# Attention, expert layer and feed-forward on one core: softmax sums and one-hot rank masks moved from VectorE to GpSimd

## The chip, the cores and the metric

The kernel runs on 1 core of a Trainium2 chip. The metric is the time of one execution on the device, in microseconds; the time before is the median of 3 runs. PE is TensorE, DVE is VectorE, ACT is ScalarE, POOL is GpSimd; SP only issues DMAs here.

## The reference

Three stages follow each other. The change touches the first, causal attention with a learned decay, and its end, where the tokens get their experts.

```python
B, H, S, D = 4, 8, 576, 64
bias = -(cum[:, :, :, None] - cum[:, :, None, :])          # cum: running sum of max(s, 0)
scores = np.where(causal, -1e9, scores + np.minimum(bias, 0.0))
attn = np.exp(scores - scores.max(-1, keepdims=True))
attn = attn / (attn.sum(-1, keepdims=True) + 1e-9)
x = attn @ v                                               # 2304 tokens x 512
...
e_idx = np.argmax(x @ w_gate, axis=1)                      # one of 8 experts per token
h = np.maximum(x[mask] @ w1[e], 0.0); ye = h @ w2[e]       # per expert, times gate weights
...
r = np.maximum(x @ w_in, 0.0); out = (r * r) @ w_out       # 512 -> 2048 -> 512
```

## The kernel before

Attention goes over 16 pairs of heads (4 batches of 4 pairs; `pp` is the pair). A pair is cut into 7 units (blocks of 128 query rows, with the last 64 rows of both heads in one unit). For each unit PE makes scores (L636), DVE adds the mask, negates and finds the row extreme (L663), ACT exponentiates and sums the rows into one column of `rs` (L680), PE transposes the weights (L696), ACT or DVE copies them out of PSUM (L715, L717). PE then multiplies with `v` (L733), in two halves of a pair: half 0 is row blocks 0 and 1, half 1 the rest. The sums of a pair lie in `rs_t[pp % 2]`, so a pair after next overwrites them.

`emit_rc` turns the sums of one half into factors: for half 1 it first moves the sums of the tail rows of the second head from partitions 64 to 127 down to 0 to 63 (L759), then adds 1e-9 (L760) and takes the reciprocal in place (L762). `emit_xe` (L806) multiplies the transposed output of the half with them, and after every fourth pair L858 uses them for the gate logits. All five are on DVE.

After each batch `emit_gate` finds each token's expert and its rank among that expert's tokens. `s_rk` (L940) gives the ranks, `s_r1` (L945) makes for each of 5 row blocks a one-hot mask of 128x384: `iota_r` (fp16) compared with the rank, written as bf16. `s_tb` (L955) multiplies the five masks with token numbers on PE: 15 small matmuls in the order of the blocks, 3 for each, which sit in PE's own order between the matmuls of the next pair. "Batch 0, 1 and 2" below are the first three of the four batches; the last batch's gate runs after attention has ended.

The order on every engine is written by hand: `at(key, fn, ...)` collects steps, and they are emitted in the order of their keys, one unit being 1.0, so that each engine executes its instructions in that order. `K_['gk']` has the keys of the gate's steps: in units after its start, the ranks at 8.68, the five masks at 9.78, 10.48, 10.95, 11.72 and 12.72, the 15 matmuls at 14.11. POOL has few other instructions in attention: for each pair a scaling of 64x128 (L521), two casts of 64x1152 that copy half a head's queries and keys (`copy_b`, L597) with a memset behind them (L598), and from pair 8 on the low half of a weight piece (`part_lo`, L273, 16 in all). The casts write a buffer that PE's scores of an earlier pair have to be done with. L580 is the low half of queries and keys, read from PSUM on DVE; PE's transposes get that PSUM bank after it.

Of the kernel before, what the change touches and what calls it, by code (L numbers as in the profile page):

```python
# [24 lines left out]
P = 128  # L25
# [4 lines left out]
K_ = dict(  # L30
    S=3,
    O=0,
    pbufs=4,
    NO=5,
    od=[-1.86, -0.33],
    lorder=[0, 2, 11, 10, 3, 1, 4],
    lvact=[[0], [1], [0], [1], [1], [0], [1, 0]],
    lpv=[[7.65, 7.66], [4.06, 5.56, 6.05, 6.9, 7.45]],
# [26 lines left out]
    rc=-0.55,  # L65
# [25 lines left out]
def attention_moe_ffn_kernel(  # L91
# [14 lines left out]
    nc = tc.nc  # L106
# [5 lines left out]
    NB = (S + P - 1) // P  # L112
    TAIL = S - (NB - 1) * P
    SP = NB * P
    HP = H // 2
    NPAIR = B * HP
# [100 lines left out]
    def at(key, fn, *args):  # L217
        tasks.append((key, len(tasks), fn, args))
# [232 lines left out]
    with tc.manual_schedule():  # L451
        with ExitStack() as actx:
# [295 lines left out]
            rc_t = {}  # L748
            xs_t = {}
            x_t = {}  # L750

            def emit_rc(pp, half):
                rs = rs_t[pp % 2]
                b, j = divmod(pp, HP)
                rc = rc_t[pp] = rc_all[b % 2][:, 2 * j:2 * j + 2]
                rsv = rs.rearrange("p (h t) -> p h t", h=2)
                b0, b1 = (0, 2) if half == 0 else (2, NB)
                if half == 1:
                    nc.vector.tensor_copy(out=rs[0:TAIL, 2 * NB - 1:2 * NB], in_=rs[P - TAIL:P, NB - 1:NB])  # L759
                nc.vector.tensor_scalar(  # L760
                    out=rc[:, :, b0:b1], in0=rsv[:, :, b0:b1], scalar1=1e-9, scalar2=None, op0=ALU.add)
                nc.vector.reciprocal(out=rc[:, :, b0:b1], in_=rc[:, :, b0:b1])  # L762

            def emit_xt(pp, half):
                j = pp % HP
# [113 lines left out]
            def emit_gate(b, tg, gk):  # L879
                last = b == B - 1  # L880
# [61 lines left out]
                def s_r1(t, c0=0, c1=CH):  # L942
                    if "r1" not in T:
                        T["r1"] = r1_p.tile([P, NB, CH * P], BF16, tag="r1", name="r1")
                    nc.vector.tensor_scalar(  # L945
                        out=T["r1"][:, t, c0 * P:c1 * P], in0=iota_r[:, c0 * P:c1 * P], scalar1=rk[:, t:t + 1], scalar2=None, op0=ALU.is_equal)

                def s_tb(c0=0, c1=CH):
# [159 lines left out]
            with tc.tile_pool(name="prep", bufs=1) as prep:  # L1108
# [19 lines left out]
                    out=mf, in_=zf[:, 0:P], pattern=[[-1, P]], compare_op=ALU.is_ge, fill=NEG, base=0,  # L1128
# [3 lines left out]
                    out=mt, in_=of[:, 0:P], pattern=[[1, P]], compare_op=ALU.is_gt, fill=0.0, base=0,  # L1132
# [7 lines left out]
                for hd in range(2):  # L1140
# [3 lines left out]
                    out=sel.unsqueeze(2), in_=ident.rearrange("p (g r) -> p r g", r=NH)[:, 0:2 * ND], axis=AX.X, op=ALU.add)  # L1144
                nc.vector.tensor_scalar(out=sq, in0=sq, scalar1=0.0, scalar2=None, op0=ALU.max)
                nc.vector.tensor_tensor_scan(
                    out=cum, data0=cum_r[0:NH].bitcast(F32), data1=sq, initial=0.0, op0=ALU.mult, op1=ALU.add)
# [4 lines left out]
                    out=cum_k[NH:2 * NH], in0=cum, in1=cum_k[0:NH].bitcast(F32), op=ALU.subtract)  # L1152
# [26 lines left out]
                for r in range(2 * ND):  # L1179
                    if r < ND:  # L1180
                        nc.scalar.activation(
                            out=cum_q[:, r], in_=cum_r.bitcast(F32), func=AF.Copy, scale=sel[:, r:r + 1])
                    else:
                        nc.gpsimd.tensor_scalar(
                            out=cum_q[:, r], in0=cum_r.bitcast(F32), scalar1=sel[:, r:r + 1], scalar2=None,
# [7 lines left out]
                    out=aug_d[1, 0:2].rearrange("c r t -> (c r) t"), in_=cum_r[0:2 * NH].bitcast(F32))  # L1193
                nc.sync.dma_start(
                    out=aug_d[1, 2:4].rearrange("c r t -> (c r) t"), in_=cum_k[0:2 * NH].bitcast(F32))
# [42 lines left out]
            def early(pp):  # L1238
                return min(NU, 3 * max(pp - ND, 0))

            for pp in range(NPAIR):
                base = NU * pp
                t0 = base - NU
                if pp >= 2:
                    at(max(t0 + K_["ldqk"] - early(pp), t0 - 2 * NU + K_["scq"] - early(pp - 2) + 0.2), load_qk, pp)
                    at(t0 + K_["ldv"], load_v, pp)
                if pp >= 1:
                    if pp >= ND:
                        at(t0 + K_["sck"] - early(pp), scale_tail, pp, nc.gpsimd)
                    else:  # L1250
                        at(K_["od"][0], scale_tail, pp, nc.vector)
                    for part in range(3):
                        tq = t0 + K_["qk"][part] - early(pp) + (0 if pp >= ND else K_["q1"])
                        at(tq, qk_pe, pp, part)
                        at(tq + K_["qkh"], qk_hi, pp, part)
                        at(tq + K_["qkl"], qk_lo, pp, part)
                if pp >= ND:
                    tb = t0 + max(K_["dup"], K_["qk"][2] + K_["qkl"] - early(pp) + 0.4)
                    at(tb - 0.05, load_aug, pp, 1)
                    at(tb - 0.04, copy_b, pp)  # L1260
                    at(tb, spread_b, pp)
                    at(tb - K_["dup"] + K_["dupa"], spread_a, pp)
                    at(tb - K_["dup"] + K_["dupa"], load_aug, pp, 0)
                end = pp == NPAIR - 1
                units, vact, pv = (K_["l" * end + nm] for nm in ("order", "vact", "pv"))
                for i, un in enumerate(units):
                    u = base + i
                    at(u - K_["LS"], emit_s, pp, un)
                    at(u - K_["LM"], emit_m, pp, un)
                    at(u - K_["LE"], emit_e, pp, un)  # L1270
                    at(u, emit_t, pp, un)
                    at(u + K_["LV"], emit_v, pp, un, vact[i])
                for half in (1, 0) if end else (0, 1):
                    for jb, tv in enumerate(pv[half]):
                        at(base + tv, emit_pv, pp, half, [jb])
                    tv = base + pv[half][-1]
                    tx = tv + K_["xe"]
                    at(tv + K_["ov"], emit_ov, pp, half, K_["ovact"][half])
                    at(tv + K_["rc"], emit_rc, pp, half)
                    at(tv + K_["xt"], emit_xt, pp, half)  # L1280
                    if end:
                        at(tx, emit_xl, pp, half)
                    at(tx + 0.001, emit_xe, pp, half)
                    if end:
                        at(tx + 0.002, store_x, pp, *((0, 2) if half == 0 else (2, NB - 1)))
                        if half == 1:
                            at(tx + 0.002, store_x, pp, NB - 1, NB)
                if end:
                    for hd in range(2):
                        for half in range(2):  # L1290
                            at(tx + 0.003, emit_xa, pp, half, hd)
                else:
                    at(tv + K_["sx"], store_x, pp, 0, NB - 1)
                    at(tv + K_["sx"], store_x, pp, NB - 1, NB)
            for b in range(B):
                last = b == B - 1
# [436 lines left out]
        with tc.For_i(0, over["end"], 1):  # L1733
            rc = lp.tile([P, B, NB], F32, tag="orc", name="orc", bufs=1)
# [4 lines left out]
            for b in range(B):  # L1739
                for t in range(NB):  # L1740
                    r1 = lp.tile([P, P], F32, tag="or1", name="or1")
                    nc.vector.tensor_scalar(
                        out=r1, in0=it_f, scalar1=rc[:, b, t:t + 1], scalar2=None, op0=ALU.is_equal)
# [3 lines left out]
                        out=vv[:, 2], in0=oh_all[:, b, t], scalar1=gsq[:, b, t:t + 1], scalar2=None, op0=ALU.mult)  # L1747
# [40 lines left out]
            for e in range(E):  # L1788
                xr = xr_p.tile([P, CH, DM], F32, tag="xr", name="xr")
                nc.gpsimd.indirect_dma_start(  # L1790
                    out=xr[:, 0, :], out_offset=None, in_=x_d[:, :],
# [8 lines left out]
                    out=out[:, :], out_offset=bass.IndirectOffsetOnAxis(ap=jx[:, e:e + 1], axis=0), in_=oo,  # L1800
# [30 lines left out]
```

## Time and profile before

| | |
|---|---|
| median of 3 runs | 860.27 us (859.9 to 860.3) |
| profiled execution, its own time | 859.34 us |
| span of its trace, first to last instruction | 857.6 us |
| granted TensorE clock | 0.997 of full speed |
| attention of the 16 pairs, about | 12 to 222 us of the span |

The span is the time from the first to the last instruction of the profiled execution. A wait is shown as `[idle before <-releaser]`: the idle time of the engine just before the instruction, and what ended it. "PEld" is the loading of weights into PE, which overlaps the matmul before it, so that an idle PEld is no idle PE. The ends of matmuls are modelled.

### The profile page before, as it was taken

Reading aid. Unit: us, or ns where it says so; the run is one execution under the profiler, and the core shown is the slowest. Engines: PE = TensorE matmul, PEld = TensorE weight load, DVE = VectorE, ACT = ScalarE, POOL = GpSimd, SP = SyncE. Lnnn points to the kernel's source line nnn. Section 1 sums busy time; section 2 is a strip of 40 time slices with the busy share of each in tenths; the row PEclk is TensorE's granted clock in tenths of the full one; section 3 lists DMA queues with packets and bytes.
Section 4 is the critical chain, followed back from the end, with each engine's and each line's share of the span. In section 5 each row is a group of like instructions: output and inputs, shape, how many; then the busy total and the mean of one; then the engine's idle time right before and its main releaser. Section 6 shows DMA issues by size and latency. Waiting matters only on the chain. (4 is left out here: it accounts for less than half of the span.)

```text
span 857.6 us, 15157 instructions
## 1 busy us (share of the span) xinstructions
PE 841.0 (98%) x5412; PEld 747.0 (87%) x5412; DVE 520.2 (61%) x1180; ACT 453.0 (53%) x1012; POOL 262.3 (31%) x304
## 2 busy tenths in 40 slices
PE   8999999999999999999999999999999999999996
PEld 6876777777799999999999999999999999999995
DVE  7667877978777677777976767664233343232221
ACT  7787878988465546665655545443233232232221
POOL 6321344543126566566422232331001011001001
PEclk9999999999999999999999999999999999999998
DMA  7676677753287888999983433321010121001001
GB/s 169 143 161 139 153 180 178 177 130 90 77 272 241 254 244 255 252 282 301 288 242 91 148 120 101 95 89 62 13 62 37 37 75 38 1 1 37 0 1 41
DMA packets 113028, 113.14 MB, mean 132 GB/s; under 512 B 66033, under 2 KB 83953, under 8 KB 112946
## 3 DMA queue, kind: packets, MB, share of 16 engines
q1 hardware_dynamic: 104962, 96.68, 42.0%
q0 software_dynamic: 3664, 9.62, 3.3%
q10 hardware_dynamic: 4320, 5.80, 2.0%
q8 instruction: 45, 0.74, 0.4%
q14 instruction: 37, 0.30, 0.1%
HBM read 80.50 MB, written 23.32 MB: 121 GB/s over the span
## 5 line engine op out<-in xcount | busy, mean ns | idle before, releaser
L1431 PE MATMUL z<-xt,w 128*128 128x384 f32 (+6 forms) x1920 | 329.6, 320 | 0.2 <-DVE h L1442 0.2
L1431 PEld LDWEIGHTS z<-xt,w 128*128 128x128 f32 x1920 | 308.1, 188 | 9.0 <-DVE h L1442 0.4
L1482 PE MATMUL z<-w,h 128*128 128x512 f32 x864 | 214.9, 393 | 0.0
L1482 PEld LDWEIGHTS z<-w,h 128*128 128x128 f32 x864 | 160.8, 188 | 29.3
L1451 DVE SCALAR_TENSOR_TENSOR r<-z,r 128x384 f32<-128x384 f32 x96 | 53.3, 556 | 127.2 <-ACT r L1450 127.0
L1450 ACT ACTIVATE r<-z 128x384 f32<-128x384 f32 x96 | 47.2, 491 | 150.6 <-PE z L1431 148.5
L1473 PE MATMUL z<-h,w 128*128 128x304 f32 (+5 forms) x768 | 111.0, 293 | 0.2 <-issue 0.2
L1473 PEld LDWEIGHTS z<-h,w 128*128 128x128 f32 x768 | 104.0, 189 | 0.7 <-issue 0.4
L1399 POOL TENSOR_TENSOR cvm<-cvm,cva 128x512 f32<-128x512 f32 x32 | 44.5, 1390 | 168.6 <-DVE cva L1395 133.7
L1541 POOL DMA_INDIRECT out_dram<-ysb,tok_m x18 | 17.4, 969 | 245.5 <-ACT ysb L1528 183.2
L1458 DVE TENSOR_TENSOR h<-r,h 128x384 fp32r<-128x384 f32 x96 | 61.0, 636 | 50.3 <-ACT h L1457 47.4
L680 ACT ACTIVATE p<-p,nm 128x128 f32<-128x128 f32 (+3 forms) x144 | 84.2, 590 | 2.6 <-DVE nm L663 2.3
L1457 ACT CAST h<-r 128x384 fp32r<-128x384 f32 x96 | 49.3, 513 | 64.0 <-DVE r L1451 63.7
L663 DVE CUSTOM_DVE_ANT_0 p<-s,mask 128x128 f32<-128x128 f32 (+3 forms) x128 | 59.7, 486 | 28.5 <-PE s L636 27.3
L250 DVE TENSOR_TENSOR w<-stg,w 128x1024 fp32r<-128x1024 f32 x49 | 73.6, 1503 | 5.4 <-ACT w L246 3.0
L696 PE MATMUL t<-ident,p 128*128 128x128 f32 x400 | 69.1, 283 | 3.2 <-DVE sta L580 1.1
L246 ACT CAST w<-stg 128x1024 fp32r<-128x1024 f32 x49 | 51.5, 1051 | 18.2 <-POOL cvm L1400 14.2
L696 PEld LDWEIGHTS t<-ident,p 128*128 128x128 f32 x400 | 44.4, 140 | 19.1 <-ACT p L680 6.2
L597 POOL CAST stb<-sta 64x1152 fp32r<-64x1152 f32 x28 | 31.4, 1149 | 78.7 <-PE s L636 46.4
L1400 POOL TENSOR_TENSOR cvm<-cvs,cvm 128x512 f32<-128x512 f32 x32 | 54.1, 1690 | 2.5
L1442 DVE SCALAR_TENSOR_TENSOR h<-z,h 128x304 fp32r<-128x304 f32 (+5 forms) x64 | 28.4, 445 | 37.4 <-ACT h L1441 29.6
L715 ACT COPY pt<-t 128x512 f32<-128x512 f32 (+1 forms) x94 | 46.9, 514 | 7.3 <-PE t L733 4.1
(242 smaller groups left out, 1043.0 us busy)
## 6 DMA issues: line engine op xcount, KB each, us to landing
stg<-in_moe_w_dram SPq DMA_DIRECT2D x42, 512.0 KB
cv<-in_moe_w_out_dram SPq DMA_DIRECT2D x16, 512.0 KB
stx<-in_moe_w_dram SPq DMA_DIRECT2D x14, 512.0 KB
cv<-in_moe_w_in_dram SPq DMA_DIRECT2D x14, 512.0 KB
xr<-yT_d SPq DMA_DIRECT2D x8, 768.0 KB
qk<-in_q_dram SPq DMA_DIRECT2D x32, 128.0 KB
v<-in_v_dram SPq DMA_DIRECT2D x32, 128.0 KB
stg<-in_moe_w_dram SPq DMA_DIRECT2D x16, 256.0 KB
```

The costliest lines, as they stand in the source:

```text
L246: nc.scalar.copy(out=w_parts(job)[0], in_=raw[job])
L250: nc.vector.tensor_tensor(out=lo, in0=raw.pop(job), in1=hi.bitcast(F32), op=ALU.subtract)
L663: nc.vector.tensor_tensor_reduce(out=dst, in0=src, in1=msk, scale=-1.0, scalar=3.0e38, op0=ALU.add, op1=ALU.min, accum_out=nm[:, c:c + 1])
L680: nc.scalar.activation(out=pt[:, cs], in_=pt[:, cs], func=AF.Exp, scale=-1.0, bias=nm[:, c:c + 1], accum_out=rs[:, r:r + 1])
L696: nc.tensor.transpose(tp[:, i * P:(i + 1) * P], pt[:, j0:j0 + P], ident)
L1400: nc.gpsimd.tensor_tensor(out=m, in0=sq, in1=m, op=ALU.add)
L1431: nc.tensor.matmul(ps[:, 0:n], lhsT=wa[:, zw, kk, fl * P:(fl + 1) * P], rhs=xt[:, zx, kk, 0:n], start=(i == 0), stop=(i == 3 * KD - 1))
L1451: nc.vector.scalar_tensor_tensor(out=gg, in0=ps[:, 0:TT], scalar=0.0, in1=gg, op0=ALU.max, op1=ALU.mult)
L1457: nc.scalar.copy(out=ht[:, 0], in_=gg)
L1458: nc.vector.tensor_tensor(out=ht[:, 1], in0=gg, in1=ht[:, 0].bitcast(F32), op=ALU.subtract)
L1473: nc.tensor.matmul(y_acc[g][d][:, 0:n], lhsT=wb[:, zw, fl, d * P:(d + 1) * P], rhs=ht[:, zh, 0:n], start=(f == 0 and i == 0), stop=(f == n ...
L1482: nc.tensor.matmul(acc, lhsT=ht[:, zh, c * P:(c + 1) * P], rhs=wb[:, zw, fl, :], start=(first and i == 0), stop=(last and i == 2))
```

## The change

In `emit_rc` the copy of the tail and the addition of 1e-9 go to POOL for all pairs but the last one. The reciprocal becomes a step of its own, `emit_ri`, and stays on DVE. The POOL part is emitted 0.3 earlier than before, the reciprocal 0.6 later than the place that all three had. The five 128x384 masks of batches 0, 1 and 2 go to POOL with their keys unchanged; the last batch's 15 smaller ones stay on DVE.

```diff
+            def emit_ri(pp, half):
+                b0, b1 = (0, 2) if half == 0 else (2, NB)
+                nc.vector.reciprocal(out=rc_t[pp][:, :, b0:b1], in_=rc_t[pp][:, :, b0:b1])
+
             def emit_rc(pp, half):
...
+                eng = nc.vector if pp == NPAIR - 1 else nc.gpsimd
                 if half == 1:
-                    nc.vector.tensor_copy(out=rs[0:TAIL, 2 * NB - 1:2 * NB], in_=rs[P - TAIL:P, NB - 1:NB])
-                nc.vector.tensor_scalar(
+                    eng.tensor_copy(out=rs[0:TAIL, 2 * NB - 1:2 * NB], in_=rs[P - TAIL:P, NB - 1:NB])
+                eng.tensor_scalar(
                     out=rc[:, :, b0:b1], in0=rsv[:, :, b0:b1], scalar1=1e-9, scalar2=None, op0=ALU.add)
-                nc.vector.reciprocal(out=rc[:, :, b0:b1], in_=rc[:, :, b0:b1])
+                if pp == NPAIR - 1:
+                    emit_ri(pp, half)
...
                 def s_r1(t, c0=0, c1=CH):
...
-                    nc.vector.tensor_scalar(
+                    (nc.vector if last else nc.gpsimd).tensor_scalar(
                         out=T["r1"][:, t, c0 * P:c1 * P], in0=iota_r[:, c0 * P:c1 * P], scalar1=rk[:, t:t + 1], scalar2=None, op0=ALU.is_equal)
...
-                    at(tv + K_["rc"], emit_rc, pp, half)
+                    at(tv + K_["rc"] - (0.0 if end else 0.3), emit_rc, pp, half)
+                    if not end:
+                        at(tv + K_["rc"] + 0.6, emit_ri, pp, half)
```

POOL's order at the masks of batch 1, before: from the token numbers (`oid_all`) that the masks' matmuls use, to the update of the running counts (`carry`).

```order
L931 TENSOR_TENSOR oid_all<-oh_all,idab 128x80
L273 TENSOR_TENSOR w_313<-stg,w_313 128x512
L521 TENSOR_SCALAR qk<-qk 64x128
L597 CAST stb_138<-sta_135 64x2x576
L597 CAST stb_138<-sta_135 64x1152
L598 MEMSET sta_135 64x576
L273 TENSOR_TENSOR w_313<-stg,w_313 128x512
L981 TENSOR_TENSOR carry<-carry,cs 128x8
```

The same place of the changed kernel, where L951 is the mask and L765 the addition:

```order
L765 TENSOR_SCALAR rca_310<-rs_157 128x2x3
L273 TENSOR_TENSOR w_313<-stg,w_313 128x512
L521 TENSOR_SCALAR qk<-qk 64x128
L951 TENSOR_SCALAR r_2423<-iota_r,rk_all 128x384
L765 TENSOR_SCALAR rca_310<-rs_156 128x2x2
L951 TENSOR_SCALAR r_2423<-iota_r,rk_all 128x384
L597 CAST stb_138<-sta_135 64x2x576
L597 CAST stb_138<-sta_135 64x1152
L598 MEMSET sta_135 64x576
L951 TENSOR_SCALAR r_2423<-iota_r,rk_all 128x384
L273 TENSOR_TENSOR w_313<-stg,w_313 128x512
L951 TENSOR_SCALAR r_2423<-iota_r,rk_all 128x384 x2
```

Two masks stand ahead of the casts. Behind the memset the third mask stands where L273 stood, then L273, then the last two masks. In batch 0 there is no L273 among them; in batch 2 there are no casts, three masks come ahead of the L273 and two behind it.

DVE's order where the gate logits of a batch are summed (once in each of the first three batches, in the fifth, ninth and thirteenth pair), before: L858 and L863 are the logits, `mask_t` is the mask of the tail unit.

```order
L863 TENSOR_REDUCE lg<-lw 128x32
L760 TENSOR_SCALAR rca_311<-rs_156 128x2x2
L762 RECIPROCAL rca_311<-rca_311 128x2x2
L663 ISA p,nm<-s_1234,mask_t 128x576
L663 ISA nm 128x1
L858 TENSOR_TENSOR lw<-t,rca_310 128x384
L863 TENSOR_REDUCE lg<-lw 128x48
L580 SCALAR_TENSOR_TENSOR sta_136<-t,sta_136 128x512
```

And in the changed kernel, where L864 and L869 are the logits and L754 the reciprocal:

```order
L869 TENSOR_REDUCE lg<-lw 128x32
L663 ISA p,nm<-s_1235,mask_t 128x576
L663 ISA nm 128x1
L864 TENSOR_TENSOR lw<-t,rca_310 128x384
L869 TENSOR_REDUCE lg<-lw 128x48
L754 RECIPROCAL rca_311<-rca_311 128x2x2
L580 SCALAR_TENSOR_TENSOR sta_136<-t,sta_136 128x512
```

The addition is gone from DVE, and the reciprocal of half 0 stands behind the tail unit's mask instead of ahead of it. In the other pairs it stands there too, directly ahead of L580.

## Rows read from the trace of the kernel before

**Rows 1.** Profile page, busy time (share of the span) of each engine.
```profile
PE 841.0 (98%) x5412; PEld 747.0 (87%) x5412; DVE 520.2 (61%) x1180; ACT 453.0 (53%) x1012; POOL 262.3 (31%) x304
```

**Rows 2.** View by windows, 80 to 150 us: width, then busy us by engine.
```profile
80.00:150.00 70.00, 68.52 (x550) 51.78 (x550) 53.57 (x200) 58.39 (x171) 24.81 (x33) 1.00 0.72 164
```

**Rows 3.** PE's waits, 24 to 225 us: total us, times, longest us.
```profile
PE t L696 <- DVE sta L580: 1.1, 2, 0.7
```

**Rows 4.** Groups by form, DVE, 20 to 225 us: busy us, mean ns.
```profile
L945 DVE TENSOR_SCALAR r<-iota_r,rk_all 128x384 bf16<-128x384 f16 x15 | 7.4, 492 | 0.0
L760 DVE TENSOR_SCALAR rca<-rs 128x6 f32<-128x6 f32 x16 | 6.0, 372 | 0.5
```

**Rows 5.** DVE's timeline, single instructions between 61 and 199 us: start, duration.
```profile
61.19 0.18 DVE L762 RECIPROCAL rca<-rca 128x4 f32<-128x4 f32 x1
61.87 0.76 DVE L663 CUSTOM_DVE_ANT_0 p<-s,mask_t 128x576 f32<-128x576 f32 x1 [0.49 <-PE s L636]
...
62.88 0.69 DVE L580 SCALAR_TENSOR_TENSOR sta<-t,sta 128x512 fp32r<-128x512 f32 x1 [0.25 <-issue]
...
75.66 0.76 DVE L663 CUSTOM_DVE_ANT_0 p<-s,mask_t 128x576 f32<-128x576 f32 x1 [0.26 <-PE s L636]
...
95.64 0.19 DVE L940 TENSOR_REDUCE rk_all<-tm 128x5 f32<-128x40 f32 x1
98.24 0.56 DVE L663 CUSTOM_DVE_ANT_0 p<-s,mask 128x384 f32<-128x384 f32 x1 [2.40 <-PE s L636]
...
99.71 1.16 DVE L945 TENSOR_SCALAR r<-iota_r,rk_all 128x384 bf16<-128x384 f16 x1
...
148.14 0.19 DVE L940 TENSOR_REDUCE rk_all<-tm 128x5 f32<-128x40 f32 x1
...
198.49 0.19 DVE L940 TENSOR_REDUCE rk_all<-tm 128x5 f32<-128x40 f32 x1
```

**Rows 6.** PE's timeline, single stretches between 104 and 207 us.
```profile
104.69 0.44 PE L696 MATMUL t<-ident,p 128*128 128x128 f32 x2 [0.38 <-DVE sta L580]
...
106.12 0.54 PE L955 MATMUL t<-oid_all,r 128*128 128x16 bf16 x15
...
154.07 0.66 PE L549 MATMUL t<-ident,qk 128*128 128x128 f32 x4 [0.49 <-DVE sta L580]
...
157.84 0.54 PE L955 MATMUL t<-oid_all,r 128*128 128x16 bf16 x15
...
205.90 0.54 PE L955 MATMUL t<-oid_all,r 128*128 128x16 bf16 x15
```

**Rows 7.** Groups by form, POOL, 14 to 225 us: busy us, mean ns.
```profile
L597 POOL CAST stb<-sta 64x1152 fp32r<-64x1152 f32 x28 | 31.4, 1149 | 78.7 <-PE s L636 46.4 <-issue 11.3 <-ACT pt L715 9.6
...
L521 POOL TENSOR_SCALAR qk<-qk 64x128 f32<-64x128 f32 x14 | 7.4, 526 | 4.0 <-DMA qk<-in_k_dram 3.6
L1184 POOL TENSOR_SCALAR cum_q<-cum_r,sel 128x576 fp32r<-128x576 f32 x2 | 3.5, 1734 | 0.1
...
L1011 POOL TENSOR_TENSOR ez<-ez,se 128x5 f32<-128x5 f32 x3 | 0.6, 200 | 0.6 <-DVE ez L1008 0.5
```

**Rows 8.** POOL's timeline, single stretches between 99 and 204 us.
```profile
99.62 2.27 POOL L597 CAST stb<-sta 64x1152 fp32r<-64x1152 f32 x2 [5.69 <-ACT pt L715]
101.94 0.58 POOL L598 MEMSET sta<- 64x576 f32 x1
...
151.04 2.27 POOL L597 CAST stb<-sta 64x1152 fp32r<-64x1152 f32 x2 [3.08 <-PE s L636]
...
154.03 1.28 POOL L273 TENSOR_TENSOR w<-stg,w 128x512 fp32r<-128x512 f32 x1
...
196.55 1.28 POOL L273 TENSOR_TENSOR w<-stg,w 128x512 fp32r<-128x512 f32 x1 [0.86 <-ACT w L269]
...
201.93 1.27 POOL L273 TENSOR_TENSOR w<-stg,w 128x512 fp32r<-128x512 f32 x1 [4.11 <-ACT w L269]
```

**Rows 9.** Timeline of PE's weight loads, one stretch in the fifth pair.
```profile
80.22 0.20 PEld L696 LDWEIGHTS t<-ident,p 128*128 128x128 f32 x2 [0.38 <-DVE sta L580]
```

## The prediction

> **What bounds the kernel now.** I read the busy shares of the page first. PE is busy for 98% of the span [rows 1], so only time in which PE waits can be won, and any instruction that makes PE wait is paid in full. The change lies wholly in attention, so I next took the view by windows over its middle: of 70 us PE is busy for 68.52, ACT for 58.39, DVE for 53.57, POOL for 24.81 [rows 2]. PE's idle time there is 1.48 us. The view of PE's waits says what it waits for: the largest DVE entry is 1.1 us in total in 24 to 225 us, behind L580 [rows 3]. The reader is to see that DVE, though it loses some 13 us of work by the change (7.4 us of masks and 6.0 us of the larger additions [rows 4]), is not what PE waits for most of the time. What has to be found is where DVE's time reaches PE, and whether POOL now does.
>
> **DVE's relief in an ordinary pair: nothing.** The sums of half 1 are handled just before DVE goes idle anyway: in batch 0 it waits 2.40 us for scores right behind them (98.24 in [rows 5]). That holds too for those of its additions that took long (the 16 have a mean of 372 ns [rows 4]): the idle time behind them is longer. The sums of half 0 stand ahead of the tail unit's mask, and there DVE waits 0.49 us for PE (61.87 in [rows 5]). Taking the addition away makes that idle time longer and starts nothing earlier. The reciprocal (0.18 us) now comes behind that mask, into the 0.25 us in which DVE waits ahead of L580 (62.88 in [rows 5]). So an ordinary pair neither gains nor loses.
>
> **The reciprocal in the three pairs with gate logits: +0.5 us.** There the 0.26 us gap ahead of the tail unit's mask (75.66 in [rows 5]) covered the reciprocal. Behind the mask come the logits' two steps and then L580 without a gap, and PE's weight loads wait 0.38 us for the next L580 [rows 9]. The 0.18 us reciprocal now lies in that full stretch: 3 x 0.18 = 0.5 us. Lower bound 0 (PE's own idle time was smaller than the 0.38 us of its loads), upper 0.5.
>
> **The price of a mask on POOL.** On DVE a mask takes 0.49 us in the mean [rows 4], and 1.16 us where a POOL cast runs at the same time (99.71 in [rows 5], 99.62 in [rows 8]). No row has this comparison on POOL. The nearest rows are POOL's TENSOR_SCALARs: 526 ns for 128 elements a partition and 1734 ns for 576 [rows 7]. The line through them is 2.70 ns an element and 0.18 us fixed, which gives 0.18 + 384 x 2.70 / 1000 = 1.22 us for a mask. Bounds: from below the cast, 1149 ns for 1152 elements [rows 7], so 0.4 us for the elements and some 0.1 us to start: 0.5 us. From above I take 2 us, the same line at nearly twice the price an element, since a comparison with two 16-bit types is in no row. I take 1.22 us because it is the same instruction with a scalar from memory. The Trainium skill, GPSIMD Engine Reference, section 4.1 Engine selection, says that one-input work on GpSimd runs roughly at line rate. The cast agrees (1.0 ns an element), the TENSOR_SCALAR rows do not; by the page the sum would be that of the third case below. The small additions I price at 0.2 us, as the smallest tensor operations (L1011 in [rows 7]).
>
> **When the masks are ready.** Five masks need 6.1 us of POOL, and POOL's order decides, so I walked the three places. Gaps between POOL instructions are 0.05 us (99.62 + 2.27 to 101.94 [rows 8]). PE needs the fifth mask only for the last 3 of 15 matmuls, that is 12/15 of 0.54 = 0.43 us after the first.
>
> Batch 0: ranks are there at 95.83 [rows 5]; POOL is idle then, so two masks and an addition are done by 98.6, ahead of the casts at 99.62. Casts and memset end at 102.52 [rows 8]. Three masks follow: 102.57 + 3 x 1.22 + 0.10 = 106.33. PE wants the fifth at 106.12 + 0.43 = 106.55 [rows 6]: in time by 0.2 us. The 0.38 us that PE waited for L580 at 104.69 [rows 6] goes, since DVE has no masks left; but PE then runs into the fifth mask, so only 0.2 us of it is kept: -0.2.
>
> Batch 1: ranks at 148.33, earlier by the long addition that goes; two masks fit ahead of the casts at 151.04, which wait for PE as before. The first instruction behind the memset starts at 154.03 [rows 8]. It is now a mask, then L273 with its 1.28 us, then two masks: 154.03 + 3 x 1.22 + 1.28 + 0.15 = 159.12. PE wants the fifth at 157.84 + 0.43 = 158.27 [rows 6]. It waits 0.85 us, and the 0.49 us stall at 154.07 that the change takes away [rows 6] only lets PE arrive earlier to wait longer. Everything behind on PE moves: +0.9. The pairs that follow have no slack to give it back.
>
> Batch 2: no casts. POOL is free at 197.83, behind L273 [rows 8]; the ranks, at 198.68 before [rows 5], come earlier by the tail copy and a long addition that sat ahead of them. Three masks and an addition end near 201.9, when the next L273 is released as before [rows 8]; it ends at 203.20, two masks follow to 205.7. PE wants the fifth at 205.90 + 0.43 = 206.33: no wait, and some of the relief stays: -0.3 (0 to 0.5).
>
> **The sum.** -0.2 + 0.9 - 0.3 + 0.5 = +0.9 us. The profiled execution took 859.34 us, 0.93 us under the median, with a span of 857.6; it would take 860.2. On the median of the runs that is 860.27 + 0.9 = 861.2 us. A measurement of this kernel can tell a difference of about 0.2%, 1.7 us: the forecast is no change that can be told. With the bounds of the mask's price alone: at 0.5 us the masks are never waited for, batch 0 gains 0.4, batch 1 its 0.5 and a little more, batch 2 0.3: with the reciprocals -0.9, 859.4. At 2 us batch 0 is late by 2.1, batch 1 by 3.2, batch 2 by about 3.2 (two masks past 204.2, an L273, two masks: 209.5), in all +9.0, 869.3. Each 0.1 us above 1.22 costs 0.3 in batch 1, from 1.3 on as much in batch 0, and from 1.4 on 0.5 in batch 2.
>
> **The rivals.**
> The forecast, a mask near 1.2 us (0.9 to 1.3): 861.2. Chance 45%.
> Slower: a mask of over 1.35 us. From there the sum passes +1.7. For it: no row has a comparison or 16-bit types in such an instruction, and the forecast has no reserve left in batch 1. Against it: both TENSOR_SCALAR rows would have to be a poor guide by a tenth and more. Mechanism: PE's 15 matmuls wait for the fifth mask in all three batches. At 1.75 us: batch 0 +1.4, batch 1 +2.5, batch 2 +1.9, reciprocals +0.5: +6.3, 866.6. Chance 21%.
> A mask at the cast's rate: 859.4, worked out above. Chance 14%.
> Faster by more: DVE's relief reaches PE through ACT in many pairs, because the true waits of PE are hidden in modelled ends. For it: DVE loses 13 us. Against it: the idle times around the removed steps. If all of PE's shown idle time of this rate (1.48 in 70 us, over 200 us: 4.2) shrank by two thirds: -2.8, 857.5. Chance 12%.
> A wait of DVE for POOL: the reciprocal stands on DVE behind an addition that POOL does in its own order, behind casts, L273 and the counts. Against it: POOL is busy for only 24.81 of 70 us [rows 2], so most additions run as soon as the sums are there, long before DVE comes to them. If one is late by 0.3 us in 10 of 30 cases, in DVE's full stretches: +3.0 on top of +0.9, 864.2. Chance 8%.
>
> **How the numbers follow.** Predicted 861.2. Faster by over 0.2% (below 858.55): the fourth case and a part of the third, 16%. Slower (above 861.99): the second, the fifth, and the upper part of the forecast, 37%. The rest, 47%, within it. For the range I leave out the dear half of the second case (above 866) and most of the fourth (below 858.2): 858.2 to 865.8.
>
> **What would show it.** Right: POOL's group of 128x384 masks has 15 of about 1.2 us; in batch 1 PE's 15 small matmuls wait for POOL's mask for about 0.5 to 1 us, in batches 0 and 2 not or for 0.2; ordinary pairs keep their length; DVE's idle time ahead of the tail unit's mask grows. Wrong: masks of 0.5 or of 1.5 us and more, a wait of DVE for POOL's addition in the list of waits, or ordinary pairs that become shorter.

## The result, and the profile after

The changed kernel takes 867.31 us (median of 6 runs, 865.32 to 867.93), the kernel before 860.10 us beside it (6 runs, 859.86 to 860.30): ratio 1.0082, 95% interval 1.0069 to 1.0095. It is 7.2 us slower; 861.2 was predicted, with 865.8 as the upper end. The profiled execution took 867.51 us with a span of 865.8, 8.2 us more than that of before. One run of e1 (4668.6 us) and one of e5 (2278.7 us), below, were slow and are left out of the comparisons.

In the changed kernel L764, L765 and L754 are the copy, the addition and the reciprocal (L759, L760, L762 before), L951 the masks, L961 their matmuls. The page's busy times, answering to [rows 1]:

```profile
PE 841.7 (97%) x5412; PEld 748.1 (86%) x5412; DVE 505.9 (58%) x1120; ACT 453.4 (52%) x1012; POOL 291.4 (34%) x364
```

DVE has lost 14.3 us, and PE has the same work as before: what was lost is idle time of PE and, as will be seen, time at a lower clock. To find the place, I took PE's 20 products with `v` of each half 1 (L733) as a mark in every pair and compared the distances of their starts in the two timelines:

| us | before | changed |
|---|---|---|
| start of the first pair's mark | 30.3 | 29.7 |
| to the second pair | 14.29 | 16.50 |
| two ordinary pairs behind it, each | 12.04, 12.03 | 12.03, 12.03 |
| the three pairs with gate logits | 14.13, 14.27, 14.13 | 14.19, 14.28, 14.20 |
| with the masks of batch 0, 1, 2 | 12.57, 12.76, 10.83 | 12.37, 13.65, 10.82 |
| last pair but one to last pair | 10.95 | 16.25 |
| last mark to the end of the span | 639.1 | 639.6 |

Nearly all of the loss is in three places: +5.3 us at the end of attention, +1.6 at its start, +0.9 at batch 1's masks. PE's waits from 24 to 235 us name them (total us, times, longest us); the long ones were not in the list of before:

```profile
PE t L852 <- DVE pt L717: 3.0, 1, 3.0
PE s L636 <- POOL qk L521: 2.0, 1, 2.0
PE t L961 <- POOL r L951: 1.9, 3, 1.0
PE t L696 <- DVE sta L580: 0.7, 1, 0.7
```

The groups of the moved instructions by form, POOL and then DVE (busy us, mean ns, idle time ahead of them), answering to [rows 4]:

```profile
L951 POOL TENSOR_SCALAR r<-iota_r,rk_all 128x384 bf16<-128x384 f16 x15 | 18.6, 1247 | 1.7 <-DVE rk_all L946 1.2
L765 POOL TENSOR_SCALAR rca<-rs 128x6 f32<-128x6 f32 x15 | 3.7, 245 | 1.3
L764 POOL COPY rs<-rs 64x1 f32<-64x1 f32 x15 | 2.7, 183 | 3.7 <-DMA xr<-x_d,idx 2.5 <-ACT p L680 0.4
...
L754 DVE RECIPROCAL rca<-rca 128x6 f32<-128x6 f32 x16 | 3.0, 186 | 6.2 <-POOL rca L765 6.1
```

A mask takes 1.25 us on POOL, and the idle column shows the loss: one of the 16 reciprocals waited 6.1 us for POOL's addition, and one copy waited 2.5 us for a transfer `xr<-x_d,idx`. That is the first gather of token rows (L303, an indirect DMA that POOL issues), in the last pair but one. POOL's timeline there, then DVE's, then PE's:

```profile
211.03 0.19 POOL L988 CAST carryb<-carry 128x8 bf16<-128x8 f32 x1
212.05 1.22 POOL L303 DMA_INDIRECT xr<-x_d,idx  x1 [0.83 <-issue]
215.75 0.18 POOL L764 COPY rs<-rs 64x1 f32<-64x1 f32 x1 [2.48 <-DMA xr<-x_d,idx]
216.02 0.25 POOL L765 TENSOR_SCALAR rca<-rs 128x6 f32<-128x6 f32 x1
```

```profile
210.08 0.08 DVE L663 DVE_READ_ACCUMULATOR2_ANT nm<- 128x1 f32 x1
216.31 0.19 DVE L754 RECIPROCAL rca<-rca 128x6 f32<-128x6 f32 x1 [6.14 <-POOL rca L765]
216.43 0.69 DVE L663 CUSTOM_DVE_ANT_0 p<-s,mask 128x512 f32<-128x512 f32 x1
...
217.15 0.68 DVE L717 COPY pt<-t 128x512 f32<-128x512 f32 x1
```

```profile
214.24 0.74 PE L834 MATMUL t<-oTx,wp 128*32 128x320 f32 x6
217.97 0.66 PE L852 MATMUL t<-ident,lgT 128*128 128x128 f32 x2 [2.99 <-DVE pt L717]
```

The gather is issued from 212.05 on; the copy behind it starts only at 215.75, the addition after it; DVE does nothing from 210.16 to 216.31, with the next scores' mask and the copy L717 that PE waits for queued behind the reciprocal; PE finishes what it has and stands for 2.99 us. In the kernel before all three steps of this half ran on DVE, and POOL's gather held up nobody; POOL went on 0.04 us behind the end of its issue:

```profile
209.66 1.21 POOL L303 DMA_INDIRECT xr<-x_d,idx  x1 [0.83 <-DVE nm L663]
210.91 0.26 POOL L986 TENSOR_TENSOR dl<-lg,mx 128x40 f32<-128x40 f32 x1
```

That makes 3.0 of the 5.3 us. Most of the rest, 2.0 us by the comparison with e3 below, is the clock. Windows of the same place (busy us by engine; the column behind POOL's is the granted clock):

```profile
214.00:216.00 2.00, 0.98 (x9) 0.22 (x7) 0.00 (x0) 0.00 (x0) 0.18 (x1) 1.00 0.43 121
216.00:218.00 2.00, 0.03 (x1) 0.06 (x1) 1.70 (x6) 0.97 (x4) 0.72 (x3) 0.69 0.00 0
218.00:220.00 2.00, 2.00 (x9) 2.00 (x10) 1.97 (x9) 1.96 (x6) 0.65 (x1) 0.50 0.03 8
220.00:222.00 2.00, 2.00 (x10) 1.92 (x10) 1.75 (x7) 0.78 (x4) 1.02 (x3) 0.50 0.49 139
222.00:224.00 2.00, 2.00 (x10) 0.82 (x9) 1.01 (x3) 0.13 (x1) 0.00 (x0) 0.60 0.00 0
```

While PE waited, its clock fell to 0.50, that is 1.2 instead of 2.4 GHz, and it stayed there while PE was fully busy again, to about 223 us. In the trace of before no stretch of 2 us between 20 and 340 us is below 0.99. The Trainium skill (TensorE: Matmul & The Clock Gate, Part 1: The HAM clock gate) says that the clock is held at the lower of two levels unless activity releases it; the trace agrees: the clock fell during the 2.99 us in which PE stood (the 0.69 of the second window puts the fall at about 216.8).

At batch 1 PE waits for masks as forecast. PE, then POOL:

```profile
158.30 0.38 PE L961 MATMUL t<-oid_all,r 128*128 128x16 bf16 x9
159.21 0.23 PE L961 MATMUL t<-oid_all,r 128*128 128x16 bf16 x3 [0.52 <-POOL r L951]
160.42 0.23 PE L961 MATMUL t<-oid_all,r 128*128 128x16 bf16 x3 [0.98 <-POOL r L951]
```

```profile
155.42 1.25 POOL L951 TENSOR_SCALAR r<-iota_r,rk_all 128x384 bf16<-128x384 f16 x1
156.64 1.28 POOL L273 TENSOR_TENSOR w<-stg,w 128x512 fp32r<-128x512 f32 x1
157.90 2.46 POOL L951 TENSOR_SCALAR r<-iota_r,rk_all 128x384 bf16<-128x384 f16 x2
```

The third place, at the start, reads in PE's timeline as a wait for POOL, but it is not one. PE, then SP's queue:

```profile
39.92 0.44 PE L636 MATMUL s<-sta 128*128 128x192 f32 x2 [1.97 <-POOL qk L521]
```

```profile
34.78 1.52 SPq L584 DMA_DIRECT2D sta<-sta  x1
36.34 0.50 SPq L539 DMA_DIRECT2D sta<-aug_d  x1
```

L521 does not write `sta`. The two transfers into it do; the first took 1.52 us to issue (0.62 before) and the second was issued 1.7 us later than before (34.64). Of that, 0.8 us come from the first, which already began later (34.78 against 33.97), and 0.9 from its long issue. The first kernel below shows the same wait under the transfer's name. How the 7.2 us between the medians divide between waits, clock and start is known only as far as the two executions of the changed kernel that were profiled (this one and e8) go.

### The profile page after: what moved, and what is told of

Read it like the earlier page. It is cut to its first block, busy times and chain, and to the rows that moved or that the text cites. A ratio compares the mean times of both kernels' runs of the same rounds, so it can differ in the third digit from the quotient of the medians.

```text
span 865.8 us, 15167 instructions
## 1 busy us (share of the span) xinstructions
PE 841.7 (97%) x5412; PEld 748.1 (86%) x5412; DVE 505.9 (58%) x1120; ACT 453.4 (52%) x1012; POOL 291.4 (34%) x364
## 5 line engine op out<-in xcount | busy, mean ns | idle before, releaser
L250 DVE TENSOR_TENSOR w<-stg,w 128x1024 fp32r<-128x1024 f32 x49 | 75.4, 1538 | 5.4 <-ACT w L246 5.4
L636 PE MATMUL s<-sta 128*64 128x288 f32 (+4 forms) x204 | 49.6, 341 | 3.8 <-POOL qk L521 2.0
L733 PE MATMUL t<-pt,v 128*64 128x320 f32 (+4 forms) x448 | 51.1, 366 | 0.0
```

The source lines that it names most:

```text
L250: nc.vector.tensor_tensor(out=lo, in0=raw.pop(job), in1=hi.bitcast(F32), op=ALU.subtract)
L733: nc.tensor.matmul(o[64 * hd:64 * hd + 64, c0:n], lhsT=vt[:, jb, hd, :], rhs=pt[:, hd, jb, c0:n], start=(jb == 0), stop=(jb == last))
```

## The experiments

Each kernel below is the changed kernel with the edit that is shown; the kernel before was timed beside them on the same chip. The ratio is estimated from the runs of both and is not the quotient of their medians.

| kernel | this, us (lowest to highest of the runs compared) | ratio to before, 95% |
|---|---|---|
| e1_pair14 | 863.0 (860.3 to 865.7) | 1.0024 (1.0014 to 1.0034) |
| e2_gather | 863.1 (861.4 to 864.3) | 1.0032 (1.0018 to 1.0047) |
| e3_sums | 864.77 (863.5 to 865.9) | 1.0057 (1.0041 to 1.0074) |
| e4_masks | 861.77 (860.4 to 863.7) | 1.0021 (1.0011 to 1.0031) |
| e5_order | 860.48 (859.7 to 861.7) | 1.0005 (0.9996 to 1.0015) |
| e6_copy | 862.23 (862.0 to 864.3) | 1.0033 (1.0021 to 1.0045) |
| e7_masks_order | 860.73 (860.0 to 862.6) | 1.0008 (0.9999 to 1.0017) |
| e8_again | 867.51 (865.1 to 868.3) | 1.0090 (1.0074 to 1.0105) |
| e9_both | 859.82 (859.2 to 861.1) | 0.9999 (0.9990 to 1.0008) |

**e1_pair14: the sums of the last pair but one on DVE.**

```diff
-                eng = nc.vector if pp == NPAIR - 1 else nc.gpsimd
+                eng = nc.vector if pp >= NPAIR - 2 else nc.gpsimd
...
-                if pp == NPAIR - 1:
+                if pp >= NPAIR - 2:
                     emit_ri(pp, half)
...
-                    at(tv + K_["rc"] - (0.0 if end else 0.3), emit_rc, pp, half)
-                    if not end:
+                    dv = pp >= NPAIR - 2
+                    at(tv + K_["rc"] - (0.0 if dv else 0.3), emit_rc, pp, half)
+                    if not dv:
```

> Only change against the changed kernel: the sums of the last pair but one (copy, addition, reciprocal) run on DVE again, at their old place. Theory (the loss is the reciprocal of that pair's half 1, which waits on DVE for a copy that POOL begins only when the first gather has landed): the last period of PE, 16.25 us in the changed kernel, goes back to about 11.0, and the time from 867.3 to about 862.0 us. Rival (additions on POOL are late in many places, and this is only the one that shows): less than half of it comes back, 865 us or more, and other waits of DVE for POOL appear.

The last distance is 10.97 us again, and the time 863.0: 4.3 us come back where 5.3 were expected. The profiled run (865.65 us) says why. It had the late transfer of the first pairs, now under its own name in PE's waits:

```profile
PE s L636 <- DMA sta<-aug_d: 2.4, 1, 2.4
```

And its clock fell behind batch 1's wait, to 0.55 and 0.59 from 162 to 166 us, so that the distance there was 13.73 instead of 12.03. The runs of this kernel sort by their mean granted clock: 860.3 and 860.8 us at 0.998, 861.5 at 0.997, and 862.6 to 865.7 at 0.995 to 0.996. (In e7 below runs at 0.995 are among the shortest, so this mean alone proves nothing; the windows of the profiled runs do.) The theory holds for the place, though not for the time; and a wait of PE has a second price, which only some executions pay.

**e2_gather: the first gather behind the sums.**

```diff
-                    at(tg + gk[16] + 0.06, gather, 0, [0])
+                    at(tg + gk[16] + 0.12, gather, 0, [0])
```

> Only change against the changed kernel: the first gather is issued behind the copy and the addition of that half instead of ahead of them; all sums stay on POOL. Theory (it is the gather ahead of them on POOL's queue): about 862.0 us, as with the sums on DVE, and no wait of the copy above 0.3 us. Rival (POOL itself is too slow for this pair, with a split of the counts, the carry and the copy ahead of it): the reciprocal still waits for 1 to 3 us, 864 to 866 us.

863.1 us, with all sums on POOL: the same as with DVE's, 1.1 above the theory's 862.0 and below the rival's 864 to 866. The copy no longer waits, the last distance is 11.47. DVE's reciprocal still waits 1.7 us for the addition, as the rival has it, but PE sees 0.5 of them. In this run too the clock fell behind the wait at batch 1:

```profile
158.00:160.00 2.00, 0.83 (x9) 0.74 (x10) 0.29 (x3) 1.25 (x4) 1.87 (x5) 0.90 0.78 185
160.00:162.00 2.00, 2.00 (x9) 1.18 (x9) 1.68 (x7) 1.20 (x2) 1.83 (x5) 0.50 0.74 178
162.00:164.00 2.00, 2.00 (x14) 1.04 (x12) 0.20 (x1) 0.20 (x2) 0.89 (x3) 0.74 0.57 143
```

The two distances from there were 14.31 and 12.97 against 13.65 and 12.04 in the changed kernel: 1.6 us.

**e3_sums and e4_masks: one half of the change each.** In e4 the condition of e1 is `pp < NPAIR`, so that all sums are where they were. The edit of e3:

```diff
-                    (nc.vector if last else nc.gpsimd).tensor_scalar(
+                    nc.vector.tensor_scalar(
```

> Only the sums are moved, all masks stay on DVE. Theory: the sums carry nearly the whole loss, and the masks some +0.7 us of it (-0.2 in batch 0, +0.9 in batch 1, 0 in batch 2), so about 866.6 us. Rival (the masks on POOL push the rest back): below 863 us.

> Only the masks of the first three batches are moved, all sums stay on DVE with their reciprocal at the old place. Theory: masks alone +0.7 us, about 861.0 us. For the 1.6 us that the changed kernel lost in its first pair, two theories: the sums on POOL cause it (then the first period here is 14.3 us and the time 861.0), or a transfer that came late by chance or for another reason (then the first period may be 16.5 us here too, and the time 862.6).

The sums alone cost 4.7 us, the masks alone 1.7, together 6.4 of the 7.2. The sums' figure is below the 866.6 expected: the profiled run (863.54 us) had the same 3.0 us wait at the end of attention and no fall of the clock, with PE empty for the whole of the second window:

```profile
212.00:214.00 2.00, 1.74 (x16) 0.57 (x15) 0.00 (x0) 0.00 (x0) 0.03 (x1) 1.00 0.49 131
214.00:216.00 2.00, 0.00 (x0) 0.00 (x0) 0.90 (x5) 0.24 (x1) 0.90 (x4) 1.00 0.00 0
216.00:218.00 2.00, 1.23 (x10) 1.26 (x11) 2.00 (x8) 1.94 (x7) 0.00 (x0) 1.00 0.00 0
```

There the last distance was 14.22, so the fall cost the changed kernel 16.25 - 14.22 = 2.0 us. The masks' figure lies above 861.0; in the profiled run (861.51 us) batch 1's distance is 13.64 as forecast, and the clock did not fall. Its first distance was 14.79, with all sums on DVE, and e3's 14.29, with the sums on POOL: neither value is the 16.5 of the late transfer, and the sums on POOL are not enough to bring it.

**e5_order: the gather as in e2, and one L273 behind batch 1's masks.**

```diff
-                at(tw + 0.5, part_lo, *job)
+                at(tw + (1.8 if i == 5 else 0.5), part_lo, *job)
```

> Against the changed kernel: the first gather behind the sums of the last pair but one, and the split of a weight piece that lay between the masks of batch 1 behind them; sums and masks stay on POOL. Theory (PE's wait of 1.5 us in batch 1 costs that wait, and in some executions a stretch at the lower clock behind it, which made the runs of the first, second and fourth kernel spread over 860 to 863): the wait goes to under 0.5 us, the clock does not fall near 160 us, the runs come together, and the time is 860.0 to 860.8 us. Rival (the spread comes from elsewhere, such as the first pairs' transfers): about 862 us with the same spread.

860.48 us, not to be told from the kernel before, with everything that the change moved still on POOL. POOL's timeline, and PE's only wait for a mask from 150 to 165 us:

```profile
154.16 3.69 POOL L951 TENSOR_SCALAR r<-iota_r,rk_all 128x384 bf16<-128x384 f16 x3
157.83 1.28 POOL L273 TENSOR_TENSOR w<-stg,w 128x512 fp32r<-128x512 f32 x1
```

```profile
PE t L961 <- POOL r L951: 0.4, 1, 0.4
```

The distance at batch 1 is 12.41 against 13.65 in the changed kernel, and the clock does not fall. The time is 2.6 us under that of e2, from which it differs by L273 alone, where the distance accounts for 1.2: the rest fits the fall that e2's profiled run paid. It was timed on another chip than e2; counted from the kernel before beside each, the difference is 2.8. One reciprocal now waits 0.64 us for POOL behind the moved L273 (at 160.2), and the distance there stays at 12.03.

**e6_copy: only the copy on DVE, the gather where it was.**

```diff
-                    eng.tensor_copy(out=rs[0:TAIL, 2 * NB - 1:2 * NB], in_=rs[P - TAIL:P, NB - 1:NB])
+                    nc.vector.tensor_copy(out=rs[0:TAIL, 2 * NB - 1:2 * NB], in_=rs[P - TAIL:P, NB - 1:NB])
```

In POOL's written order the changed kernel has, behind the gather, a copy that waits for a software transfer (DMASW); here the addition stands in its place and waits for DVE's copy only:

```
L303 DMA xr<-x_d,idx_92 128x512 [waits DMAHW4_49,DMAHW5_49,DMAHW2_49,DMAHW7_49,DMAHW0_49,DVE_49]
L764 COPY rs_156<-rs_156 64x1 [waits DMASW0_49,Pool_49]
L765 TENSOR_SCALAR rca_311<-rs_156 128x2x3 [waits Pool_49]

L303 DMA xr<-x_d,idx_92 128x512 [waits DMAHW4_49,DMAHW5_49,DMAHW2_49,DMAHW7_49,DMAHW0_49,DVE_49]
L765 TENSOR_SCALAR rca_311<-rs_156 128x2x3 [waits DVE_49]
```

> Against the changed kernel: only the copy of the tail's sum runs on DVE, the addition stays on POOL, in the same place behind the first gather. In the written order the addition then has no wait for a software transfer. Theory (what cost was the landing of the gather, on which the copy waited, not its place in the queue): the addition runs right behind the issue of the gather, near 211.3 us, PE's wait of 3.0 us goes, about 863 us as with the gather behind. Rival (any instruction of POOL behind the gather begins only when it has landed): the addition begins near 215 us again, 866 to 867 us.

```profile
211.64 1.21 POOL L303 DMA_INDIRECT xr<-x_d,idx  x1 [0.83 <-issue]
212.93 0.25 POOL L765 TENSOR_SCALAR rca<-rs 128x6 f32<-128x6 f32 x1
```

862.2 us. The addition starts 0.08 us behind the end of the issue. The rival is out: POOL goes on behind a gather; it was the copy's written wait that held it until the rows had landed. Standing behind the gather in the queue costs DVE 3.2 us of waiting here, but PE only 0.5 (11.50 against 10.95). The copy does not need the rows: on DVE, emitted in the same place, it runs at 209.30, before the gather is issued. Why it is given that wait on POOL when it follows the gather, and not when it precedes it, the runs do not show.

**e7_masks_order: masks alone with that L273 behind them.** The edits of e4, and of e5 the one shown.

> Only the masks on POOL, with the split of the weight piece behind batch 1's; all sums on DVE. Theory: without the wait in batch 1 the masks on POOL cost nothing, -0.2 us in batch 0 and up to -0.3 in batch 2: 859.8 to 860.3 us, no change that can be told from the kernel before. Rival (DVE's relief of 7 us reaches PE once no mask is waited for): under 859 us.

860.73 us: 0.4 above the theory's range, with an interval that just holds no change; the rival is out. Of the forecast gains batch 0 shows 0.1 us (12.48 against 12.57) and batch 2 none (10.84 against 10.83). PE waits for the masks of batch 1 for 0.4 us and the distance is 12.39.

**e8_again: the changed kernel once more.**

> The changed kernel once more, unchanged, to see which of its losses come back: the wait of 3.0 us in the last pair but one and the 1.5 us in batch 1 should (both theories of them are in the written order); the late transfer of the second pair (2.0 us) and the stretch at half clock near 218 to 223 us need not. If both stay away the profiled run is near 864, if both come it is near 867.5 us.

867.51 us; the profiled run, 865.11 us, had the two waits for POOL, and not the late transfer (first distance 14.29). The clock fell at the end of attention again, for a shorter time:

```profile
PE t L852 <- DVE pt L717: 3.1, 1, 3.1
PE t L961 <- POOL r L951: 1.9, 3, 1.0
```

```profile
216.00:218.00 2.00, 1.00 (x6) 1.04 (x6) 2.00 (x10) 1.71 (x6) 0.00 (x0) 0.59 0.00 0
218.00:220.00 2.00, 2.00 (x11) 1.93 (x10) 1.93 (x8) 1.76 (x6) 1.28 (x1) 0.56 0.50 143
```

The last distance was 14.99.

**e9_both: both mends, the first by DVE.** The edits of e1, and of e5 the one shown.

> The changed kernel with both mends: all sums of the last pair but one on DVE, the split of the weight piece behind batch 1's masks. Theory (with its two waits gone the change neither costs nor gives, DVE's relief being idle time): 860.0 to 860.5 us, no difference to the kernel before that can be told; PE waits for masks 0.5 us in batch 1, and the last period is 11.0 us, against 11.46 with the gather behind the sums. Rival (the relief of 13 us on DVE is worth something once nothing is waited for): under 859 us.

859.82 us, ratio 0.9999: no difference, as the theory has it, 0.2 under its range. The distances at batch 1 and at the end are 12.41 and 10.97. DVE is busy for 504.9 us, 15.3 less than before, and it is worth nothing that can be told.

## Why the prediction was wrong

**Ordinary pairs, "neither gains nor loses": right.** They keep 12.03 to 12.04 us, and e9 shows the same for the whole: DVE's relief was idle time, and the fourth rival (the relief reaches PE) is out. Ahead of the tail unit's mask it grew, as forecast, from 0.49 us [rows 5] to 0.79:

```profile
63.41 0.76 DVE L663 CUSTOM_DVE_ANT_0 p<-s,mask_t 128x576 f32<-128x576 f32 x1 [0.79 <-PE s L636]
```

**Reciprocals behind the gate logits, +0.5: right in sign, too large.** The three pairs grew by 0.06, 0.01 and 0.07 us, 0.14 in all, inside the bounds of 0 to 0.5. With the sums alone moved (e3) they are 14.19, 14.28, 14.19, with the masks alone (e4) 14.13, 14.28, 14.14.

**Price of a mask, 1.22 us: right** (1.25 us, 15 times). The Trainium skill (GPSIMD Engine Reference, 4.1 Engine selection) has one-input work at roughly line rate. At the rate of the cast, the row nearest to that, a mask would take the 0.5 us of the prediction's third case; the trace disagrees by a factor of 2.5. The third case of the prediction (masks at the cast's rate) and the second (over 1.35 us) are out.

**Batch 0, -0.2: right (-0.20), in part by luck.** The 0.38 us wait for L580 went as forecast, but PE waited 0.39 us for the fifth mask, twice the forecast, and some 0.2 us won elsewhere in that stretch made up for it:

```profile
107.82 0.23 PE L961 MATMUL t<-oid_all,r 128*128 128x16 bf16 x3 [0.39 <-POOL r L951]
```

**Batch 1, +0.9: right (+0.89)** in its direct part, by the walk as written: L273 between the masks, the fifth mask late. The fourth was late too, so that PE waited 0.52 and 0.98 us; the 0.49 us wait for L580 went as forecast. **Batch 2, -0.3: wrong**, -0.01; its masks were in time, but the shorter work on DVE did not reach PE.

These terms, with the reciprocals, sum to +0.8 where +0.9 was forecast. They were the terms of the prediction, and they are not where the time went.

**The step that failed is the dismissal of the last rival**, "a wait of DVE for POOL", which had a chance of 8%. The prediction put against it that "POOL is busy for only 24.81 of 70 us [rows 2], so most additions run as soon as the sums are there". Most did. But the share comes from 80 to 150 us, and it counts busy time; the issue of the gather and the wait for its landing stand elsewhere, at 212 us, and are waiting. POOL's queue was walked at the masks of three batches and not at the sums of all 15 pairs, so that the gather ahead of the last pair but one's copy was never met; a wait of DVE for POOL's addition was one of its own signs of being wrong. The rival was also sized as many small delays ("0.3 us in 10 of 30 cases"); it was a single one of 6.1 us on DVE, 3.0 on PE. e1 and e2 show the place, e6 the wait behind it.

**The price of a wait of PE was sized by its length alone.** The prediction has no term for the clock, which is to put it at nothing without a reason. At the end of attention the fall cost 2.0 us on top of the wait (the changed kernel against e3), and behind batch 1's wait, which costs 0.9, it cost 1.7 us in e1 and 1.6 in e2, and nothing in four other profiled runs with the same wait (the changed kernel twice, e4, e6). The masks alone cost 1.7 us in e4 and 0.5 in e7, with 0.4 us of batch 1's wait left; that is 1.2 us, the distance's share, and the 0.5 that is left is no more than a measurement can tell.

**The start, +1.6 in the profiled run, is not shown to be the change's.** The late transfer came in 2 profiled runs (the changed kernel and e1) and stayed away in a second run of the very same kernel (e8) and in e3, with the same sums on POOL. Five other kernels had first distances of 14.7 to 15.1 us, four of them with a wait of PE of 0.2 to 0.4 us in the same place, and of the kernel before there is one trace. What makes SP's queue late in some executions stays open.

## What to carry to other kernels

When a step is moved to another engine's queue, write down what stands directly ahead of each of its instances there, DMA issues and their waits too; a share of busy time over some other stretch cannot answer that, and one late instance out of thirty made most of the loss here. A wait that stops the bounding engine is not paid by its length alone: look for a granted clock below 1.00 in the windows behind it. And a relief of an engine that idles ahead of each of its waits was worth nothing here (13 us of DVE), so that the move could only be neutral or lose.

## What the runs showed of the hardware

The fall of the clock is not certain. Of three profiled runs with a wait of 3.0 to 3.1 us at the end of attention (the changed kernel, e3, e8) it fell in two, to 0.50 over some 7 us in one and to 0.56 to 0.59 over two windows of 2 us in the other. Of six that waited 0.5 (e6: 0.8) and 1.0 us with 0.23 us of work between at batch 1 (the changed kernel, e1, e2, e4, e6, e8) it fell in two. In the profiled runs without such a wait (before, e5, e7, e9; PE's longest there is 0.8 us) no stretch of 2 us between 20 and 340 us is below 0.99.

An indirect DMA of 128 rows of 512 elements keeps POOL for 1.22 us; its rows are there about 2.4 us after that. The Trainium skill (DMA: Bandwidth & Descriptors, Anatomy of one DMA — SWDGE (gpsimd) path) gives 2.0 us for setup and completion plus the bytes over 436 GB/s for a DMA that GpSimd issues, an estimate of 2.6 us for these 256 KB. The idle time ahead of the copy, from the end of the issue, is 2.48 us; from the start of the issue to the copy it is 3.70 us, 1.1 above the estimate, so the trace agrees only if the issue is left out.

The two DVE means of [rows 4] mix two prices. Of the 16 additions of 128x6 in the trace of before the ten that no L273 on POOL overlapped took 170 to 175 ns, the six that one did took 297 to 1052 ns: about 3.2 of their 6.0 us are that slowdown (an estimate, the six less six times 172 ns). On POOL the addition took 245 ns in the mean. Of the 15 masks nine took 290 to 313 ns, with POOL idle, and the six that a cast or an L273 overlapped 526 to 1164 ns; on POOL each took 1.25 us. One addition of either kind, and the L273 beside the second:

```profile
83.02 0.17 DVE L760 TENSOR_SCALAR rca<-rs 128x6 f32<-128x6 f32 x1
...
171.25 1.05 DVE L760 TENSOR_SCALAR rca<-rs 128x6 f32<-128x6 f32 x1
...
170.99 1.29 POOL L273 TENSOR_TENSOR w<-stg,w 128x512 fp32r<-128x512 f32 x1 [2.50 <-ACT w L269]
```

Other DVE instructions kept their time beside an L273, the copy of the sums for one (149 ns with and without). Why some are slowed and others not, no run here shows.
